# Linformer attention feeding a maxout layer: two products of batch 0 moved ahead of the first up product, and one projection moved to another PSUM bank

## The chip, the cores and the metric

The kernel runs on one core of one Trainium2 chip. A core has a matrix engine (TensorE, in the profile PE, with its weight loads as PEld), a vector engine (VectorE, DVE), a scalar engine (ScalarE, ACT), a general one (GpSimd, POOL) and a queue engine (SyncE, SP). Each runs its own list of instructions in order; they wait for each other through semaphores. TensorE writes into PSUM, which this kernel divides into eight banks. The metric is the device time of one execution in microseconds (us); the time before is 332.01 us, the median of nine runs (329.39 to 332.21).

## The reference

Eight batches, eight heads, 1024 positions, head size 64. Keys and values are projected along the sequence to 64 rows, then comes ordinary attention over these 64, and the heads side by side (8192 rows of 512) go into a two-branch maxout layer:

```python
k_proj = einsum('ks,bhsd->bhkd', E, k)
v_proj = einsum('ks,bhsd->bhkd', F, v)
attn = softmax(q @ k_proj.T / 8)
x = (attn @ v_proj), heads side by side      # 8192 x 512
g = maximum(x @ w1, x @ w2)                  # 8192 x 1024
out = g @ w_out                              # 8192 x 512
```

## The kernel before

**Algebra.** max(a, b) is relu(a - b) + b. So with wd = w1 - w2 and m = w2 @ w_out, the output is relu(x @ wd) @ w_out + x @ m. wd is made by VectorE in four pieces of 256 columns (`step_wd`, L418), m by TensorE from transposed w2 (`step_w2t` L427, `step_m` L440). "Up" is x @ wd with relu, "down" the product with w_out and m. Batch 0 does its up products plainly (`up_slots`, L404): 16 blocks u0[0..7] and u1[0..7], four matmuls of 512 columns each; u0 reads the first 256 columns (j = 0) of each half of x, u1 the second (j = 1). From batch 1 on, up and down use seven block products in place of eight (`up_steps` L558, `down_steps` L636).

**Attention of one batch.** `step_kv` projects k and v (L180), `step_kpt` and `step_qt` transpose (L211, L237) for batches 0 and 1; later batches have their q transposed by DMA (L249). Heads are taken in two groups g of four, positions in two parts j. For a pair (g, j): `step_sc` gives scores (L266) and their exponentials (L306), `step_dn` sums and logarithms of sums (L278, L312), `step_inv` their inverses (L316), and `step_at` the products with v (L278: 16 small matmuls) and the multiplies by the inverses (L329: two per pair) that write x, called xt. Later batches do the same in `step_group`.

**PSUM.** Four single banks, mm0 to mm3, are given out in rotation by `mm_bank()`; later they are named outright. Two double banks, the attention banks, come from `att_banks()`. `step_kv` and `step_at` take a flag `att`, which says from which of the two. With it, `step_kv` hands back its second half (the eviction of v, L196, and its copy, L200), to be issued after the next slot.

**Order.** The whole order is written out by hand. Lines L717 to L751 are batch 0's attention. Then a list `slots` gives the order of batch 0's up products, the w2 transposes, the m products and all later work; a second table hangs attention steps of the next batch behind given slots. Filler matmuls on a matrix of ones (`warm(n)`, L140) are issued at places of the first stage; nobody reads their result. `loads(1, "v", "q", "k")` issues three loads of later batches on POOL's queue (L102); v and q of batch 2 are loaded behind batch 1's `step_kv`. Stores (L651) and the DMA transposes (L249) share SP's queue.

Around the change, the program order of batch 0 is: products for (0, 0), products for (1, 0), the first piece of wd, u0[0], products for (0, 1), u0[1], products for (1, 1), three loads, the second piece of wd, u1[0], u1[1], u0[2], and so on.

Of the kernel before, what the change touches and what calls it, by code (L numbers as in the profile page):

```python
# [16 lines left out]
def kernel(  # L17
# [14 lines left out]
    B, H, S, D = q.shape  # L32
# [27 lines left out]
    def mm_bank(dtype=FP32, n=None):  # L60
        if n is None:
            n = turn.pop(0)
            turn.append(n)
        return ps.tile([128, 512 if dtype == FP32 else 1024], dtype, tag=f"mm{n}", name="mm_ps")

    def att_banks(dtype=FP32):
        return ps.tile(
            [128, 2, 512 if dtype == FP32 else 1024], dtype, tag="att", bufs=2, name="att_ps"
        )
# [27 lines left out]
    def load_all(t, b, n, src):  # L97
        alloc(t, n)
        load(t, n, src, b, 0, H)
# [37 lines left out]
    def warm(n):  # L137
        w_ps = mm_bank()
        for _ in range(n):
            nc.tensor.matmul(  # L140
                out=w_ps, lhsT=ones16[:, 0:128], rhs=ones16, start=True, stop=True
            )
# [145 lines left out]
    def values_into(t, g, j, at_ps):  # L288
        for z in range(2):
            tiles_into(  # L290
                lambda o: at_ps[o][:, z * W : (z + 1) * W], t["ex", g, j],
                lambda rows, hh: t["vp"][rows, 4 * g + hh, z, :],
            )

    def new_xt(t):
        t["xt"] = xpool.tile([128, NP2, 2, HALF], FP16, tag="xt", name="xt_sb")

    def x_out(t, g, j):
        return t["xt"][:, 2 * g : 2 * g + 2, :, j * W : (j + 1) * W]
# [18 lines left out]
    def step_at(t, g, j, att=False):  # L318
        if "xt" not in t:
            new_xt(t)  # L320
        ld = t.pop(("ld", g, j))
        if att:
            both = att_banks()
            at_ps = [both[:, o, :] for o in range(2)]
        else:
            at_ps = [mm_bank() for _ in range(2)]
        values_into(t, g, j, at_ps)
        for o in range(2):
            nc.vector.tensor_tensor(  # L329
                out=x_out(t, g, j)[:, :, o, :],  # L330
                in0=at_ps[o].rearrange("q (z n) -> q z n", z=2),
                in1=ld[:, o, None, :].broadcast_to([128, 2, W]),
                op=ALU.mult,
            )
# [63 lines left out]
    def up_slots(t, j):  # L398
        t["gt", j] = gt = gpool.tile([128, NFB, HALF], FP16, tag="gt", name="gt_sb")
        for fb in range(NFB):  # L400
            def up(fb=fb):
                h_ps = mm_bank()
                for r in range(NDC):
                    nc.tensor.matmul(  # L404
                        out=h_ps,
                        lhsT=wd_sb[:, r, fb * 128 : (fb + 1) * 128],
                        rhs=t["xt"][:, r, :, j * W : (j + 1) * W],
                        start=(r == 0), stop=(r == NDC - 1),
                    )
                if fb < 3:  # L410
                    nc.scalar.activation(out=gt[:, fb, :], in_=h_ps, func=ACTF.Relu)
                else:
                    nc.vector.tensor_scalar_max(gt[:, fb, :], h_ps, 0.0)
            yield up


    def step_wd(f0):
        nc.vector.tensor_tensor(  # L418
            out=wd_sb[:, :, f0 : f0 + 256], in0=w1_sb[:, :, f0 : f0 + 256],
            in1=w2_sb[:, :, f0 : f0 + 256], op=ALU.subtract,  # L420
        )

    def step_w2t(f0):
        ps_t = mm_bank(FP16)
        for f in range(2):
            for r in range(NDC):
                nc.tensor.transpose(  # L427
                    out=ps_t[:, (f * NDC + r) * 128 : (f * NDC + r + 1) * 128],
                    in_=w2_sb[:, r, f0 + f * 128 : f0 + (f + 1) * 128],
                    identity=ident16,  # L430
                )
        fb = f0 // 128
        nc.scalar.copy(
            out=w2t_sb[:, fb : fb + 2, :].rearrange("q f m -> q (f m)"), in_=ps_t
        )
# [281 lines left out]
    t = tiles[0]  # L717
# [31 lines left out]
    step_inv(t, 1, 1)  # L749
    step_at(t, 1, 0)  # L750
    step_wd(0)  # L751


    load_all(tiles[1], 1, "k", k)
    u0, u1 = [*up_slots(t, 0)], [*up_slots(t, 1)]
    wt = [lambda f0=f0: step_w2t(f0) for f0 in range(0, DF, 256)]
    wd = [lambda f0=f0: step_wd(f0) for f0 in range(0, DF, 256)]
    f = lambda s, *a: lambda: s(tiles[0], *a)

    def loads(b, *names):  # L760
        for n in names:
            b_ = b + (n == "k" and b < 2)
            if b_ < B:
                load_all(tiles[b_], b_, n, {"k": k, "v": v, "q": q}[n])

    slots = [
        (0, u0[0]), (None, f(step_at, 0, 1)), (1, u0[1]), (None, f(step_at, 1, 1)),
        (None, lambda: loads(1, "v", "q", "k")),
        (None, wd[1]), (2, u1[0]), (3, u1[1]), (4, u0[2]), (None, wt[0]), (5, u0[3]),
        (None, wd[2]), (None, wt[1]), (6, u1[2]), (7, u1[3]), (8, u0[4]), (9, u0[5]), (None, wd[3]),  # L770
        (None, wt[2]), (10, u1[4]), (11, u1[5]), (12, u0[6]), (13, u0[7]), (None, wt[3]),
        (14, u1[6]), (15, u1[7]),
# [28 lines left out]
    def at_slot(key, s, *a):  # L801
        steps.setdefault(key, []).append(lambda: s(*a))
# [11 lines left out]
    t = tiles[1]  # L814
    at_slot((0, 19), new_attn, t)
    at_slot((0, 19), lambda: turn.__setitem__(slice(None), [2, 3]))
    for n, x in enumerate((
        "kv", "", "kpt", "qt00 qt10", "", "sc00 sc10", "qt01", "qt11", "",
        "dn00 in00 dn10 in10", "", "", "at00 AT10 sc01", "", "",
    )):  # L820
        key = ("P", 0, (n - 1) // 2, (n - 1) % 2) if n else (0, 19)
        for name in x.split():
            if name[0] == "k":
                if name == "kpt":
                    at_slot(key, step_kpt, t, 0, H, True)
                else:
                    at_slot(key, step_kv, t)
                    at_slot(key, loads, 2, "v", "q")
            else:
                g, j = int(name[2]), int(name[3])  # L830
                s_ = {"qt": step_qt, "sc": step_sc,
                      "dn": step_dn, "in": step_inv, "at": step_at, "AT": step_at}[name[:2]]
                args = (4 * g, 4, 2 * j, 2 * j + 2) if name[:2] == "qt" else (g, j)
                at_slot(key, s_, t, *args, *([True] if name[:2] == "AT" else []))
        if n in (1, 5):
            at_slot(key, step_t, 1, (0, 1) if n == 1 else (2, 3))
        if 6 <= n < 10:
            at_slot(key, sums_x, U[0, 1], ((2, 0, 1, 3)[n - 6],))


    t = tiles[2]
# [8 lines left out]
    for b in range(3, B):  # L850
        t = tiles[b]
# [75 lines left out]
```

## Time and profile before

| | |
|---|---|
| median of nine runs | 332.01 us |
| profiled execution, its own time | 330.6 us |
| span in the profile (first to last instruction) | 328.8 us |
| TensorE busy | 318.0 us, 97% |
| VectorE busy | 239.6 us, 73% |
| ScalarE busy | 201.0 us, 61% |
| mean granted TensorE clock | 0.994 |
| DMA queues | 53.14 MB moved, mean 162 GB/s |

The page gives busy time, the chain of work that ended last, and the groups of instructions by line. A row of the timeline has the start in us from the span's start, a length, the engine, the line, the operation with its tiles, a count, and in brackets how long the engine stood idle before it and what ended that. A row with a count covers its instructions from the first start to the last end; small matmuls overlap in it. A table by stretches gives each engine's busy time, then the granted clock and the DMA share. Landing times count from the issue of a load on its queue.

### The profile page before, as it was taken

The numbers are of one execution on the slowest core, as the hardware profiler recorded it, in microseconds if no ns is written. First come the engines' busy times: TensorE is split into PE (matmuls) and PEld (weight loads), VectorE is DVE, ScalarE is ACT, GpSimd is POOL, SyncE is SP. The second block draws the span as 40 slices with busy tenths as digits, with TensorE's granted clock in tenths as the row PEclk, the third lists the DMA queues.
The fourth block names the chain that finished last, engine by engine and source line by source line (L and its number), as shares of the span: only waits on it lengthen the run. The fifth ranks groups of instructions, "written<-read, shape, count | busy, mean of one in ns | idle before, by whom it ended". The sixth has DMA issues, their size and how long they took to land.

```text
span 328.8 us, 9007 instructions
## 1 busy us (share of the span) xinstructions
PE 318.0 (97%) x3852; PEld 248.7 (76%) x3852; DVE 239.6 (73%) x424; ACT 201.0 (61%) x359; POOL 37.2 (11%) x56
## 2 busy tenths in 40 slices
PE   7986999999999999999999999999999999999994
PEld 3542546777888788878887888878887888888883
DVE  1246698995968779677968787777967796969572
ACT  2263422566776577767776677667776777765541
POOL 8555002003000030003000200003000000000000
PEclk9899999999999999999999999999999999999999
DMA  8999999997997789995999799897999220212132
GB/s 151 202 199 202 208 207 199 207 221 132 193 243 168 152 123 225 196 212 89 203 236 198 101 172 242 199 175 106 221 189 211 64 99 32 98 34 98 33 129 96
DMA packets 74680, 53.14 MB, mean 162 GB/s; under 512 B 29456, under 2 KB 74512, under 8 KB 74640
## 3 DMA queue, kind: packets, MB, share of 16 engines
q0 software_dynamic: 29376, 28.31, 54.6%
q1 hardware_dynamic: 45264, 24.25, 30.4%
q8 instruction: 30, 0.49, 0.6%
q14 instruction: 10, 0.08, 0.1%
HBM read 57.15 MB, written 16.78 MB: 225 GB/s over the span
## 4 chain that ended last, share of the span: by engine, by line
PE 89%; DVE 6%; DMA 2%; issue 1%; ACT 1%; SPq 0%; DVEq 0%
PE mm_ps L636 43%; PE mm_ps L558 25%; PE mm_ps L404 4%; PE att_ps L180 3%; PE att_ps L278 3%; PE mm_ps L266 3%; PE mm_ps L440 2%; PE mm_ps L180 2%; DMA big<-in_F_dram 2%; PE mm_ps L140 1%; DVE xt_sb L329 1%; DVE qt_sb L242 1%; DVE gt_sb L573 1%; DVE o_sb L660 1%; PE mm_ps L237 1%
## 5 line engine op out<-in xcount | busy, mean ns | idle before, releaser
L529 ACT COPY p_sb<-mm_ps 128x512 f32<-128x512 f32 x172 | 97.2, 594 | 43.0 <-PE mm_ps L558 30.6
L636 PEld LDWEIGHTS <-big 128*128 128x128 f16 x768 | 73.6, 98 | 12.0 <-issue 3.5
L636 PE MATMUL mm_ps<-T_sb,big 128*128 128x256 f16 x576 | 77.9, 273 | 0.0
L573 DVE TENSOR_TENSOR gt_sb<-mm_ps,p_sb 128x512 f16<-128x512 f32 x56 | 38.5, 688 | 45.8 <-PE mm_ps L558 42.6
L558 PE MATMUL mm_ps<-big,big 128*128 128x256 f16 x336 | 50.4, 273 | 0.0
L558 PEld LDWEIGHTS <-big 128*128 128x128 f16 x448 | 43.8, 98 | 5.3 <-issue 0.2
L636 PEld LDWEIGHTS <-gt_sb 128*128 128x128 f16 x384 | 35.7, 98 | 9.6 <-issue 5.4
L636 PE MATMUL mm_ps<-wo_sb,gt_sb 128*128 128x256 f16 x256 | 42.9, 273 | 0.1
L558 PEld LDWEIGHTS <-wd_sb 128*128 128x128 f16 x336 | 32.9, 98 | 4.2 <-issue 0.4
L558 PE MATMUL mm_ps<-xt_sb,wd_sb 128*128 128x256 f16 x224 | 33.6, 272 | 0.2 <-ACT ex_sb L355 0.2
L355 ACT ACTIVATE ex_sb<-mm_ps 128x512 f16<-128x512 f32 x50 | 27.2, 597 | 9.6 <-PE att_ps L278 7.0
L381 DVE TENSOR_TENSOR xt_sb<-att_ps,ld_sb 128x1024 f16<-128x1024 f32 x26 | 31.7, 1219 | 0.1
L660 DVE TENSOR_TENSOR o_sb<-mm_ps,p_sb 128x512 f32<-128x512 f32 x32 | 21.9, 684 | 11.0 <-PE mm_ps L636 7.6
L636 PE MATMUL mm_ps<-m_sb,xt_sb 128*128 128x256 f16 x128 | 24.4, 273 | 0.0
L608 ACT ACTIVATE gt_sb<-mm_ps 128x512 f16<-128x512 f32 x28 | 16.8, 600 | 8.7 <-PE mm_ps L558 8.7
L519 DVE TENSOR_TENSOR big<-gt_sb 128x1024 f16<-128x1024 f16 x32 | 21.9, 684 | 0.2
L576 DVE TENSOR_SCALAR gt_sb<-gt_sb 128x512 f16<-128x512 f16 (+1 forms) x56 | 20.4, 365 | 1.9
L636 PE MATMUL mm_ps<-T_sb,gt_sb 128*128 128x256 f16 x128 | 21.5, 273 | 0.0
L636 PE MATMUL mm_ps<-wo_sb,big 128*128 128x256 f16 x128 | 21.5, 273 | 0.0
L636 PEld LDWEIGHTS <-xt_sb 128*128 128x128 f16 x192 | 18.8, 98 | 2.2
L229 POOL COPY junk<-kpt_sb 1x1 f16<-1x1 f16 x5 | 0.9, 176 | 164.6 <-DMA kpt_sb<-kp_sb 164.6
L573 DVE TENSOR_TENSOR gt_sb<-p_sb 128x512 f16<-128x512 f32 x28 | 19.1, 681 | 0.0
(87 smaller groups left out, 429.2 us busy)
## 6 DMA issues: line engine op xcount, KB each, us to landing
out_dram<-o_sb SPq DMA_DIRECT2D x63, 256.0 KB, 2.5
k_sb<-in_k_dram POOLq DMA_DIRECT2D x7, 1024.0 KB, 10.1
v_sb<-in_v_dram POOLq DMA_DIRECT2D x7, 1024.0 KB, 17.5
q_sb<-in_q_dram POOLq DMA_DIRECT2D x7, 1024.0 KB, 22.5
k_sb<-in_k_dram POOLq DMA_DIRECT2D x4, 256.0 KB, 6.9
q_sb<-in_q_dram POOLq DMA_DIRECT2D x4, 256.0 KB, 8.0
v_sb<-in_v_dram POOLq DMA_DIRECT2D x2, 512.0 KB, 11.8
big<-in_moe_w_dram POOLq DMA_DIRECT2D x8, 128.0 KB, 9.8
```

Source lines behind the costliest of these rows:

```text
L180: nc.tensor.matmul(out=kv_ps[r * KP : (r + 1) * KP, 0:n], lhsT=eft[:, i, c, :], rhs=t[w][:, h0:h1, c, :], start=(c == 0), stop=(c == NC - 1),)
L355: nc.scalar.activation(out=t["ex", g, j][:, e, :], in_=banks[e], func=ACTF.Exp, scale=scale)
L381: nc.vector.tensor_tensor(out=x_out(t, g, j).rearrange("q z o n -> q o z n"), in0=at_ps.rearrange("q o (z n) -> q o z n", z=2), in1=ld[:, ...
L404: nc.tensor.matmul(out=h_ps, lhsT=wd_sb[:, r, fb * 128 : (fb + 1) * 128], rhs=t["xt"][:, r, :, j * W : (j + 1) * W], start=(r == 0), stop= ...
L519: nc.vector.tensor_tensor(out=S(i), in0=x, in1=y, op=op)
L529: copy(out=x, in_=bank)
L558: nc.tensor.matmul(out=bank[:, m * W : (m + 1) * W], lhsT=w_[:, n_, (2 * d + m) * 128 : (2 * d + m + 1) * 128], rhs=a[:, n_, :], start=(n ...
L573: nc.vector.tensor_tensor(out=c_blk(j, c), in0=two(x), in1=two(y), op=ALU.add)
L576: nc.vector.tensor_scalar_max(ap, ap, 0.0)
L608: nc.scalar.activation(out=out, in_=in_, func=ACTF.Relu)
L636: nc.tensor.matmul(out=bank[:, i * CH : (i + 1) * CH], lhsT=a(c)[:, i * 128 : (i + 1) * 128], rhs=w_(c), start=(n is not None and m == (lo ...
L660: nc.vector.tensor_tensor(out=o_sb, in0=two(x), in1=two(y), op=ALU.add)
```

## The change

The products of (0, 1) and (1, 1) are taken out of the slots and issued at the end of batch 0's attention, behind the first piece of wd in program order and ahead of u0[0]; they write attention banks in place of four rotating ones. Four filler matmuls follow them. The loads and the second piece of wd keep their places relative to their own engines' work: the order on VectorE, ScalarE, POOL and SP is the same as before. Batch 1's `step_kv` takes an attention bank too; its second half is issued one slot later.

```diff
     step_at(t, 1, 0)
     step_wd(0)
+    step_at(t, 0, 1, True)
+    step_at(t, 1, 1, True)
+    warm(4)
...
     slots = [
-        (0, u0[0]), (None, f(step_at, 0, 1)), (1, u0[1]), (None, f(step_at, 1, 1)),
-        (None, lambda: loads(1, "v", "q", "k")),
-        (None, wd[1]), (2, u1[0]), (3, u1[1]), (4, u0[2]), (None, wt[0]), (5, u0[3]),
+        (0, u0[0]), (1, u0[1]), (None, lambda: loads(1, "v", "q", "k")), (2, u1[0]), (3, u1[1]),
+        (None, wd[1]), (4, u0[2]), (None, wt[0]), (5, u0[3]),
...
-                    at_slot(key, step_kv, t)
+                    at_slot(key, step_kv, t, 0, H, "kv", True)
```

## The prediction

> **What bounds the kernel now.** I read the page first (busy shares, then the chain that ended last), then the timelines of TensorE and VectorE around the edit, then every arrival that work after the edit depends on.
>
> ```profile
> PE 318.0 (97%) x3852; PEld 248.7 (76%) x3852; DVE 239.6 (73%) x424; ACT 201.0 (61%) x359; POOL 37.2 (11%) x56
> PE 89%; DVE 6%; DMA 2%; issue 1%; ACT 1%; SPq 0%; DVEq 0%
> ```
>
> TensorE is the bound: busy 97% of the span, 89% of the chain. Whatever shortens its idle time early moves all later work, unless something on a clock of its own (a transfer) takes over. The edit lies where the page still shows gaps. The timeline of TensorE there (start, length, group, idle before it):
>
> ```profile
> 24.12 0.41 PE L278 MATMUL mm_ps<-ex_sb,vp_sb 64*32 64x256 f16 x16 [0.72 <-DVE vp_sb L193]
> 26.62 1.04 PE L404 MATMUL mm_ps<-xt_sb,wd_sb 128*128 128x512 f16 x4 [2.09 <-DVE wd_sb L418]
> 27.59 0.41 PE L278 MATMUL mm_ps<-ex_sb,vp_sb 64*32 64x256 f16 x16
> 27.93 1.04 PE L404 MATMUL mm_ps<-xt_sb,wd_sb 128*128 128x512 f16 x4
> 28.90 0.41 PE L278 MATMUL mm_ps<-ex_sb,vp_sb 64*32 64x256 f16 x16
> 29.48 0.59 PE L404 MATMUL mm_ps<-xt_sb,wd_sb 128*128 128x512 f16 x2 [0.17 <-DVE xt_sb L329]
> 30.79 2.32 PE L404 MATMUL mm_ps<-xt_sb,wd_sb 128*128 128x512 f16 x10 [0.72 <-DVE xt_sb L329]
> ```
>
> It idles 2.09 us until VectorE has made the first quarter of wd (L418); only then come the two last products with v (L278, at 27.59 and 28.90), each behind an up product (L404). The third up product, u1[0], needs the multiplies of those very products and waits 0.17 and 0.72 us. From 30.79 on TensorE runs without a gap until 57.9. VectorE shows the same from its side:
>
> ```profile
> 25.88 0.68 DVE L418 TENSOR_TENSOR wd_sb<-big,big 128x1024 f16<-128x1024 f16 x1
> 28.14 2.60 DVE L329 TENSOR_TENSOR xt_sb<-mm_ps,ld_sb 128x512 f16<-128x512 f32 x4 [1.58 <-PE mm_ps L278]
> 30.66 0.68 DVE L418 TENSOR_TENSOR wd_sb<-big,big 128x1024 f16<-128x1024 f16 x1
> ```
>
> After wd it stands 1.58 us for the late products, then needs 2.60 us for the four multiplies; their end, 30.74, releases 30.79.
>
> **The change, part by part.**
>
> *Products with v ahead of the first up product.* Both go into the gap. Their inputs are ready: the attention pairs they write were last read by ScalarE's L312, which ended at 22.3 and 24.4. After the block at 24.12, issued by about 24.46, two blocks at 0.34 each (27.59 to 27.93) end near 25.2. The first up product still waits for wd: 26.62, unchanged. VectorE's order is unchanged too, so the multiplies now follow wd at once: 26.56 + 2.60 = 29.16. TensorE meanwhile needs from 26.62 two up products at 0.865 (the x10 row: the next group begins 2.16 us later, 0.216 each), to 28.35, and the first half of u1[0], to 28.78; it then waits 0.4 us for the multiplies and takes the second half at 29.2 instead of 30.79. **Gain 1.6 us.** Counted on TensorE: 2 x 0.45 of products taken out from between the up products (1.31 from 26.62 to 27.93 less 0.865), plus 0.17 and 0.72 of waits with some 0.2 of refilling around them, less the 0.4 that stays.
>
> *Next on VectorE*, wd's second quarter moves from 30.66 to about 29.1, and is needed by u0[2], now at 29.2 + 0.43 + 0.865 = 30.5. Its last weights were issued at 21.55 and took 5.9 us: 27.5, in time. It now falls beside POOL's load issue of 29.14 to 30.01. Row: the first wd piece ran at 25.88 while POOL issued without a break (25.10 to 27.80) and took 0.68 like the one at 38.97 with POOL idle. The Trainium skill (SBUF — State Buffer, "Who interferes with whom") has a rule against this edit: a VectorE operation with two SBUF inputs contends for a shared port pair with a GpSimd instruction reading SBUF, and the loser blocks fully. If issuing counted as that, wd would end at 30.01 + 0.68 = 30.7, u0[2] would start 0.25 late, and the gain be 1.35. I take the row: no loss.
>
> *Four dummies* (L140): 4 x 0.216 = 0.87 us, from 25.2 to 26.1, half a microsecond before 26.62. Covered by the wait for wd; without that cover they would cost 0.87, at half clock 1.73 (then ending near 27.0, 0.3 late). What can they bring? The rows of granted clock:
>
> ```profile
> 6.00:8.00 2.00, 1.86 (x11) 1.07 (x10) 0.68 (x1) 0.24 (x1) 2.00 (x4) 0.93 1.20 180
> 8.00:10.00 2.00, 2.00 (x9) 1.17 (x8) 0.00 (x0) 0.34 (x1) 1.18 (x3) 0.50 1.20 191
> 10.00:12.00 2.00, 2.00 (x16) 0.60 (x15) 0.71 (x2) 0.00 (x0) 1.38 (x2) 0.72 1.24 204
> 25.00:26.00 1.00, 0.00 (x0) 0.00 (x0) 1.00 (x3) 0.47 (x1) 1.00 (x3) 1.00 1.38 200
> ```
>
> (Stretch, length, busy times of PE, PEld, DVE, ACT, POOL, then the granted clock.) Across the gap the clock stayed at 1.00, so here they bring 0. The skill (TensorE: Matmul & The Clock Gate, Part 1) has the clock halved after an idle window of about 3.4 us in a free-running count; a 2.09 us gap is shorter, so its rule also gives 0. But the dip of 7 to 11 us contradicts it as a limit: half clock although TensorE was busy 1.86 of 2 us just before. That dip cost 0.14 + 1.00 + 0.56 = 1.7 us of clock, so in executions with another phase the gap may cost up to that. Bounds for the dummies: 0 to 1.7 us gained; I take 0 (the 25:26 row is nearest).
>
> *v, q and k loads.* Same order on POOL, past the same instructions; they wait for buffers free since 23.2. SP's queue keeps its order. Nothing.
>
> *Batch 1's k and v into an attention bank.* The same 16 products (1.89 us at 51.3) into a bank whose last reader, a multiply of the last products, ends at 29.2. The evictions (kp 0.58, vp 0.69, its copy 0.75) keep order; the second half is issued one slot later in program order, behind products that sit on another engine. Before, the bank was one of the rotation, and the transposes of q at about 56.0 waited for its eviction, over at 54.5: a wait removed that had ended. The rotation's phase shifts, each bank still reused after three others. 0 us, bounds -0.1 to +0.2 (the only idle near: 0.18 at 58.50, on a qt copy).
>
> *Do later arrivals allow it?* With all of TensorE 1.6 us earlier:
>
> ```profile
> q_sb<-in_q_dram POOLq DMA_DIRECT2D x1, 1024.0 KB, 24.7
> 55.53 1.06 PE L237 MATMUL mm_ps<-ident,q_sb 128*128 128x128 f16 x16
> 77.63 0.18 POOL L229 COPY junk<-qt_sb 1x1 f16<-1x1 f16 x1 [22.44 <-DMA qt_sb<-q_sb]
> 79.80 0.40 PE L266 MATMUL mm_ps<-qt_sb,kpt_sb 64*32 64x256 f16 x16
> ```
>
> Batch 1's q was issued at 28.02 and lands at 52.7; wanted at 55.53, then at 53.9: 1.2 spare. Batch 1's v lands at 26.86 + 20.8 = 47.7, wanted at 51.3, then 49.7. Batch 2's v and q are issued sooner (53.45 to 51.9) but queue behind k, which lands at 29.14 + 28.6 = 57.7, so q still lands at 69.9 and the transposed q at about 77.6; its first scores move from 79.80 to 78.2: **0.6 spare, the narrowest place**. Beyond it, loads for batch 3 start behind that gate and are read past 100 us.
>
> *Sum.* -1.6 + 0 + 0: span 328.8 to 327.2, the profiled execution 330.6 to 329.0. The nine runs before have a median of 332.01, 1.4 above the profiled one; the same difference gives **330.4**.
>
> **Rivals.**
>
> (a) *Transfers take the gain.* Loads kept the DMA engines full until 70 us. If in the usual 332 us execution batch 2's q lands a microsecond or more later than here, 79.80 doesn't move fully; gain 0 to 0.6, time 331.4 to 332.0. For: 0.6 spare. Against: TensorE would be later there too, and keep its distance.
>
> (b) *The gap costs clock in the usual execution.* The 1.4 us between profiled run and median would be a half-clock stretch caused by the gap; the dummies end it. Gain 1.6 + 1.4, time 329.0. For: the dip can cost 1.7 and changes phase freely. Against: not seen at the gap in this profile.
>
> (c) *Slower: half-clock stretches elsewhere.* The new order makes TensorE's activity fall otherwise on the clock's count, in the up products from 26.6 on. Price 1.7 each: one gives 332.1 (no change), two 333.8. Slower from 1.6 + 1.0 = 2.6 us of lost clock. Against: clock 1.00 in every row after 12 us, with more idle time than the new order has.
>
> (d) *It doesn't do what it says.* If the multiplies came later on VectorE, or a product waited for an attention pair, 332.0. The compiled order has the products directly behind the last block, the multiplies directly behind wd.
>
> **How the numbers follow.** Main case 0.60 (own range 329.7 to 331.0: port rule, spare time, spread of runs); (a) 0.12; (b) 0.10; (c) 0.15, of which 0.04 ends within no change; (d) 0.03. What a measurement here can tell from no change is 0.3%, 1.0 us. Faster: 0.60 of the main case less 0.04 for runs falling short, plus (b), plus 0.02 of (a): 0.68. Same: 0.04 + 0.10 + 0.04 + 0.03 = 0.21. Slower: the rest of (c), 0.11. Range 328.7 to 332.5: from (b) to just past one dip.
>
> **What would show it.** Right: the products at 24.5 to 25.2, dummies behind, the first up product still at 26.6, the multiplies at 26.5 to 29.2, one wait of some 0.4 us inside u1[0], then no gap; everything from there 1.6 us earlier, the scores at 78.2 without a wait. Wrong: the first up product after 26.7, wd's second piece over 0.7, a wait for qt near 78, or granted clock below 1.00 after 12 us.

## The result

The changed kernel takes 329.14 us (median of 18 runs, 327.75 to 331.13) where the kernel before takes 331.95 us (median of 55 runs): ratio 0.993, 95% interval 0.9913 to 0.9947, so 2.3 us faster, between 1.8 and 2.9. The forecast was 330.4, a gain of 1.6; the direction and the range held, the size was short by 0.7 us in the ratio and by 1.3 us in the median.

### The profile after

Its profiled execution took 327.73 us with a span of 326.0. The page's busy shares and its chain (shares of the span):

```profile
PE 317.4 (97%) x3856; PEld 248.9 (76%) x3856; DVE 239.5 (73%) x424; ACT 201.0 (62%) x359; POOL 37.0 (11%) x56
PE 86%; DMA 6%; DVE 4%; POOL 2%; issue 1%; ACT 1%; DVEq 0%; POOLq 0%
```

TensorE does the same work, and the four dummies, in a shorter span. In the chain, 6% now runs over transfers, where it was 2%: loads of batch 0's v (4%) and of the weights (2%), issued ahead of the edit. The timeline of TensorE around the edit:

```profile
22.99 0.41 PE L278 MATMUL mm_ps<-ex_sb,vp_sb 64*32 64x256 f16 x16 [0.52 <-DVE vp_sb L193]
23.22 0.62 PE L278 MATMUL att_ps<-ex_sb,vp_sb 64*32 64x256 f16 x32
23.77 1.04 PE L140 MATMUL mm_ps<-ones 128*128 128x512 f16 x4
25.50 4.71 PE L404 MATMUL mm_ps<-xt_sb,wd_sb 128*128 128x512 f16 x20 [0.68 <-DVE wd_sb L418]
30.04 0.61 PE L427 MATMUL mm_ps<-ident,big 128*128 128x128 f16 x8
```

The two moved blocks are the x32 row at 23.22, the dummies follow, and the first five up products run as one group. The first w2 transpose of the kernel before was here:

```profile
32.95 0.61 PE L427 MATMUL mm_ps<-ident,big 128*128 128x128 f16 x8
```

From the products of (1, 0) to the first w2 transpose it is 30.04 - 22.99 = 7.05 us; before, 32.95 - 24.12 = 8.83. I call this distance *the stretch*. It is **1.78 us** shorter. VectorE over the same time:

```profile
24.75 0.68 DVE L418 TENSOR_TENSOR wd_sb<-big,big 128x1024 f16<-128x1024 f16 x1
25.35 2.48 DVE L329 TENSOR_TENSOR xt_sb<-att_ps,ld_sb 128x512 f16<-128x512 f32 x4
27.75 0.68 DVE L418 TENSOR_TENSOR wd_sb<-big,big 128x1024 f16<-128x1024 f16 x1
```

The 1.58 us in which it stood for late products are gone, and the second piece of wd, beside POOL's load issues of 27.83 to 29.64, still takes 0.68.

The two spans differ by 2.8 us, but 1.1 of that is not the change: the products of (1, 0) start 1.13 us earlier already, ahead of anything that was edited. The granted clock accounts for it (columns as in the prediction, then the DMA share and GB/s):

```profile
6.00:8.00 2.00, 2.00 (x13) 1.20 (x12) 0.69 (x1) 0.08 (x1) 2.00 (x4) 1.00 1.19 188
8.00:10.00 2.00, 2.00 (x16) 0.98 (x16) 0.42 (x1) 0.51 (x1) 1.73 (x3) 1.00 1.23 199
24.00:26.00 2.00, 1.32 (x7) 0.47 (x6) 2.00 (x5) 0.16 (x1) 2.00 (x3) 1.00 1.41 199
```

This execution has no dip to half clock at 8 to 11 us, and the second projection of k already runs 1.4 us earlier (13.48 against 14.85); 0.3 is then lost to a wait for v's load. The code up to there is the same in both kernels, so that is chance from one execution to the next. Comparing the two profiles end to end would mistake it for part of the gain.

Farther on, the lines that answer to the arrivals in the prediction:

```profile
q_sb<-in_q_dram POOLq DMA_DIRECT2D x1, 1024.0 KB, 24.6
52.62 1.06 PE L237 MATMUL mm_ps<-ident,q_sb 128*128 128x128 f16 x16
76.94 0.18 POOL L229 COPY junk<-qt_sb 1x1 f16<-1x1 f16 x1 [24.64 <-DMA qt_sb<-q_sb]
76.90 0.40 PE L266 MATMUL mm_ps<-qt_sb,kpt_sb 64*32 64x256 f16 x16
```

Batch 1's q (issued at 27.83, landed at 52.4) was there 0.2 us before its transposes at 52.62. Here almost nothing is left to spare. Batch 2's first scores (the last line) started 2.9 us earlier than before and without a wait. That the gate (L229) opened at the same moment means nothing for them: it reads the last head, and the first scores need only the first four (see the account below).

### The profile page after: what moved, and what is told of

Its sections match the earlier page's. It is cut to its first block, busy times and chain, and to the rows that moved or that the text cites. A ratio compares the mean times of both kernels' runs of the same rounds, so it can differ in the third digit from the quotient of the medians.

```text
span 326.0 us, 9015 instructions
## 1 busy us (share of the span) xinstructions
PE 317.4 (97%) x3856; PEld 248.9 (76%) x3856; DVE 239.5 (73%) x424; ACT 201.0 (62%) x359; POOL 37.0 (11%) x56
## 4 chain that ended last, share of the span: by engine, by line
PE 86%; DMA 6%; DVE 4%; POOL 2%; issue 1%; ACT 1%; DVEq 0%; POOLq 0%
PE mm_ps L636 43%; PE mm_ps L558 26%; DMA v_sb<-in_v_dram 4%; PE att_ps L180 4%; PE mm_ps L404 4%; PE att_ps L278 3%; PE mm_ps L266 3%; PE mm_ps L440 2%; DMA big<-in_moe_w_dram 2%; POOL q_sb L102 1%; POOL k_sb L102 1%; DVE gt_sb L573 1%; DVE o_sb L660 1%; PE mm_ps L427 1%; DVE qt_sb L242 0%
## 5 line engine op out<-in xcount | busy, mean ns | idle before, releaser
L229 POOL COPY junk<-kpt_sb 1x1 f16<-1x1 f16 x5 | 0.9, 177 | 162.5 <-DMA kpt_sb<-kp_sb 162.5
```

## The experiments

**What was to be told apart.** Theory A: the gain is the multiplies that follow wd at once, 1.6 to 1.8 us. Theory B, the prediction's rival (b): part of it is clock that the gap used to cost. Theory C: part of it is the other bank for batch 1's projection. P stands for the moved products, D for the four dummies, K for the projection's bank; the changed kernel is P+D+K. Ratios are to the kernel before, timed beside each experiment on the same chip. *Lost clock* is one minus the mean granted clock, times the span, as a mean over a kernel's runs; over 144 runs the kernel before lost 2.31 us, over 19 runs the changed one lost 0.95.

Lost clock is a sign, not a price: part of it lies where TensorE has nothing to do. The changed kernel's profile lost about 1 us of clock, all of it behind the last matmul, which ended at 321.6:

```profile
324.00:325.00 1.00, 0.00 (x0) 0.00 (x0) 0.00 (x0) 0.00 (x0) 0.00 (x0) 0.50 0.27 93
```

Over the 144 runs of the kernel before, a straight line through time and lost clock has a slope of 0.42 us per us.

### P alone

```diff
     step_wd(0)
     step_at(t, 0, 1, True)
     step_at(t, 1, 1, True)
-    warm(4)
...
-                    at_slot(key, step_kv, t, 0, H, "kv", True)
+                    at_slot(key, step_kv, t)
```

(This diff is against the changed kernel.)

> The two products ahead of the first up product, in attention banks; no dummies, batch 1's projection in its old bank. Theory A (the whole gain is the multiplies that follow the first piece of wd without a gap): as fast as the changed kernel, 1.6 to 1.8 us under the kernel before, ratio 0.9945 to 0.9955. Theory B (part of the measured 2.3 us is clock that the dummies save in the gap): only 0.8 to 1.2 us, ratio 0.996 to 0.998. Theory C (the attention bank for the projection brings the rest): 1.8 us at most, with the projection's own run showing what is missing.

Measured: 329.44 us, ratio 0.9923 (0.9893 to 0.9952), lost clock 1.38 us over 10 runs, stretch 7.04 us. The products alone carry a gain as large as that of the whole change. Theory B's smaller figure for this run is outside the interval; theory A's lies just inside it.

### D alone

```diff
     step_wd(0)
+    warm(4)
```

(Against the kernel before.)

> The kernel before with four dummies behind the first piece of wd, ahead of the first up product, and nothing else. Theory A: they lie in the wait for wd (2.09 us for 0.87 us of work), 0 us, ratio 1.000. Theory B: they keep the clock up in the usual execution, 0.5 to 1.5 us faster, ratio 0.9955 to 0.9985.

Measured: 331.29 us, ratio 0.9989 (0.9964 to 1.0014); lost clock only 0.47 us over 14 runs, stretch 8.82 us. The dummies do save clock, about 1.8 us of it, but the time hardly moves. The interval leaves both theories open; the next experiment doubles the number of dummies.

### D with eight dummies

```diff
     step_wd(0)
+    warm(8)
```

(Against the kernel before.)

> The kernel before with eight dummies (1.73 us) in the 2.09 us gap ahead of the first up product, and nothing else: the dummies' effect with twice the dose. Theory B: mean lost clock falls from 2.7 us to under 0.6 us, and since a half-clock stretch behind the gap cost 1.0 us where a profile showed one, the time falls by 0.6 to 1.3 us, ratio 0.996 to 0.998. Theory A: lost clock may fall, the time stays, ratio 0.999 to 1.001.

Measured: 331.21 us, ratio 0.9985 (0.997 to 1.0001), lost clock 0.69 us over 22 runs. Again clock saved with little to show for it. The timeline of TensorE in this kernel tells where it goes:

```profile
51.01 0.38 PE L180 MATMUL mm_ps<-k_sb,eft 128*64 128x512 f16 x1 [0.67 <-ACT m_sb L444]
```

Batch 1's projection waits 0.67 us for ScalarE's copy of the last m block. The dummies take one rotating bank, which turns the rotation by one, and the projection, which takes a fixed bank (number 2), now gets the one that the last m product has just filled. The same wait stands in the profile with four dummies. Before, it got another m block's bank, long empty.

### K alone

```diff
-                    at_slot(key, step_kv, t)
+                    at_slot(key, step_kv, t, 0, H, "kv", True)
```

> The kernel before with batch 1's projection of k and v in an attention bank, its second half one slot later, and nothing else. Theory A: 0 us, ratio 1.000, since the wait that it removes had ended 1.5 us before it was asked for. Theory C: 0.5 to 1 us faster, ratio 0.997 to 0.9985.

Measured: 332.02 us, ratio 1.0011 (0.9985 to 1.0037). Alone the bank is worth nothing, as theory A had it. Its profile had a chance find, in the stretches of 2 us:

```profile
24.00:26.00 2.00, 0.30 (x2) 0.19 (x3) 1.64 (x3) 0.34 (x1) 2.00 (x3) 1.00 1.42 200
26.00:28.00 2.00, 2.00 (x23) 0.67 (x22) 0.78 (x2) 0.60 (x1) 2.00 (x3) 0.78 1.23 201
28.00:30.00 2.00, 2.00 (x20) 0.43 (x19) 0.99 (x2) 0.60 (x1) 1.84 (x3) 0.50 1.18 175
30.00:32.00 2.00, 1.48 (x7) 0.55 (x6) 1.40 (x3) 0.51 (x1) 0.00 (x0) 0.87 1.20 160
```

This kernel has the old gap of 2.09 us, and behind it, in the up products, the clock falls to half. The early dip is missing here. Its stretch is 9.81 us, 0.98 longer than the 8.83 of the kernel before at full clock: what rival (b) described does happen, and the profile of before had merely not caught it.

### D and K together

```diff
     step_wd(0)
+    warm(4)
...
-                    at_slot(key, step_kv, t)
+                    at_slot(key, step_kv, t, 0, H, "kv", True)
```

(Against the kernel before.)

> The kernel before with the four dummies and batch 1's projection in an attention bank; the products stay where they were. In the two runs with dummies alone the dummies' bank turned the rotation by one, and the projection then waited 0.67 us for the last m copy, which hid a gain in clock. Theory B': without that wait the dummies are worth 0.5 + 0.67, 0.8 to 1.4 us: ratio 0.996 to 0.9975, mean lost clock under 0.8 us, no wait ahead of the projection. Theory A (dummies worth nothing): ratio 0.999 to 1.001.

Measured: 330.38 us, ratio 0.9959 (0.9944 to 0.9974), lost clock 0.88 us over 22 runs, no wait ahead of the projection; stretch 8.83 us, unchanged. So without moving a product, dummies and bank are worth 1.4 us (0.9 to 1.9). The stretch at full clock is no shorter, which makes the clock the likeliest thing that they bring. The profiled execution can't show it: at 331.57 us it was one of this kernel's slowest, with the early dip and a wait far behind the edit, for a transposed k:

```profile
223.80 0.41 PE L266 MATMUL mm_ps<-qt_sb,kpt_sb 64*32 64x256 f16 x16 [0.93 <-DMA kpt_sb<-kp_sb]
```

Five of the fourteen profiles have this wait, of 0.9 to 1.1 us (here, and with P alone, D alone, one product moved, and rotating banks with dummies). How often each kernel meets it was not measured, so it stays open as a part of the differences between kernels.

### P and D, the projection in a rotating bank

```diff
-                    at_slot(key, step_kv, t, 0, H, "kv", True)
+                    at_slot(key, step_kv, t)
```

(Against the changed kernel.)

> The changed kernel with batch 1's projection back in a rotating bank (products and dummies as changed). The five banks taken less turn the rotation as the dummies alone do, so the projection waits 0.67 us for the last m copy: 0.5 to 0.7 us slower than the changed kernel, ratio 0.9945 to 0.9955, the wait seen in the profile. If the bank does not matter: ratio 0.992 to 0.994 and no wait.

Measured: 329.62 us, ratio 0.9939 (0.9915 to 0.9963), stretch 7.05. The interval doesn't separate it from the changed kernel, but the profile has the wait that was expected, and a second one:

```profile
PE mm_ps L180 <- ACT m_sb L444: 0.7, 1, 0.7
PE mm_ps L237 <- DMA q_sb<-in_q_dram: 0.5, 1, 0.5
```

(Who waited for what: us in total, times, longest.) The first is the bank. The second is batch 1's q, which landed at 54.6 here; TensorE had to wait for it even after losing 0.7 us.

### P and K, no dummies

```diff
     step_at(t, 1, 1, True)
-    warm(4)
```

(Against the changed kernel.)

> The changed kernel without its four dummies. Theory A (multiplies alone): ratio as the changed kernel, 0.993 to 0.9945, stretch from the first products of (1, 0) to the first transpose of w2 7.05 us as there. Theory B (gap costs clock): the products themselves fill 0.4 us of the gap, so some of the clock comes back: mean lost clock (one minus the granted clock, times the span) between the 0.95 us of the changed kernel and the 2.7 us of the kernel before, and 0.2 to 0.5 us slower than the changed kernel, ratio 0.9935 to 0.996.

Measured: 329.31 us, ratio 0.992 (0.9889 to 0.9951), lost clock 1.97 us over 8 runs. The profile shows the gap's dip once more:

```profile
25.88 6.00 PE L404 MATMUL mm_ps<-xt_sb,wd_sb 128*128 128x512 f16 x20 [1.65 <-DVE wd_sb L418]
```

And the stretches of 2 us around it:

```profile
24.00:26.00 2.00, 0.35 (x22) 0.12 (x2) 2.00 (x4) 0.61 (x2) 2.00 (x4) 0.89 1.39 197
26.00:28.00 2.00, 2.00 (x6) 0.62 (x6) 2.00 (x4) 0.19 (x1) 2.00 (x3) 0.50 1.26 202
28.00:30.00 2.00, 2.00 (x9) 0.85 (x8) 0.82 (x2) 1.00 (x2) 2.00 (x3) 0.76 1.12 156
```

A gap of 1.65 us suffices for it, and the same 20 matmuls take 6.00 us instead of 4.71: 1.29 us. Yet over its runs this kernel is no slower than the changed one. With 8 runs and an interval of 1 us to either side, the 0.2 to 0.5 us that was expected can't be seen or denied.

### Only one of the two products moved

```diff
     step_at(t, 0, 1, True)
-    step_at(t, 1, 1, True)
...
-        (0, u0[0]), (1, u0[1]), (None, lambda: loads(1, "v", "q", "k")), (2, u1[0]), (3, u1[1]),
+        (0, u0[0]), (1, u0[1]), (None, f(step_at, 1, 1, True)), (None, lambda: loads(1, "v", "q", "k")), (2, u1[0]), (3, u1[1]),
```

(Against the changed kernel.)

> The changed kernel, but only the products of (0, 1) stand ahead of the first up product; those of (1, 1) follow the second up product. Theory A: VectorE does two of the four multiplies early and the other two about 28.7 to 30.0 on the time scale of the profile before, so u1[0] gets its second half at 30.1 instead of 29.2 or 30.8: 0.7 us under the kernel before, ratio 0.998. Theory B or C (the gain is not in the multiplies): close to the changed kernel, ratio 0.993 to 0.995.

Measured: 330.19 us, ratio 0.995 (0.9935 to 0.9965), 1.7 us, with 0.66 us of lost clock over 22 runs; stretch 8.38 us. The stretch at full clock is only 0.45 us shorter than before (0.7 was expected: the second product comes behind the second up product and its multiplies wait for it). The time gained is larger than the stretch by 1.2 us, and this kernel too has the gap filled with dummies: about what dummies and bank bring on their own (1.4). Theory A's ratio of 0.998 lies outside the interval.

### 20 dummies

```diff
-    warm(4)
+    warm(20)
```

(Against the changed kernel.)

> The changed kernel with 20 dummies in place of four: 16 x 0.216 = 3.46 us more in TensorE's order, of which 0.7 us fit into the rest of the gap and 0.2 us into the wait inside u1[0]. If the dummies are free only by their cover: 2.5 us slower than the changed kernel, ratio to the kernel before 1.000 to 1.002. If something later (a load) takes up part of the delay: less, ratio 0.996 to 0.999.

Measured: 330.92 us, ratio 0.9992 (0.9976 to 1.0007), stretch 9.43 us: 2.4 longer than in the changed kernel, 2.0 us in the ratio. Dummies are free only as long as the wait for wd covers them; beyond that nearly their whole length is paid.

### The moved products in rotating banks, with and without dummies

```diff
-    step_at(t, 0, 1, True)
-    step_at(t, 1, 1, True)
+    step_at(t, 0, 1)
+    step_at(t, 1, 1)
```

(Against the changed kernel; the second run leaves out `warm(4)` as well.)

> The changed kernel with the two moved products written into rotating banks, as before, in place of attention banks. The first two up products then reuse banks that the multiplies of (0, 1) have to empty: they start about 0.6 us later and follow VectorE, which still ends its multiplies at the same time. Theory A: 0.2 to 0.4 us slower than the changed kernel, ratio 0.994 to 0.996. If the attention banks are the essence of the change: most of the gain gone, ratio over 0.997.

> The two products moved into rotating banks, no dummies, projection in an attention bank. In the run with dummies the dummies' own bank had to wait for a multiply, which held the up products back. Without them the first up product waits for the first multiply of (0, 1), about 0.5 us past wd, and u1[0] ends 0.3 us later than in the changed kernel: stretch from the products of (1, 0) to the first transpose of w2 7.3 to 7.5 us at full clock against 7.05, ratio 0.993 to 0.996. If the attention banks matter by themselves: ratio over 0.997.

Measured with dummies: 331.42 us, ratio 0.9991 (0.9969 to 1.0014), nearly all of the gain gone; the expectation was wrong. Its timeline of TensorE:

```profile
22.97 0.63 PE L278 MATMUL mm_ps<-ex_sb,vp_sb 64*32 64x256 f16 x32 [0.52 <-DVE vp_sb L193]
24.27 0.27 PE L278 MATMUL mm_ps<-ex_sb,vp_sb 64*32 64x256 f16 x1 [0.67 <-DVE xt_sb L329]
24.87 0.41 PE L278 MATMUL mm_ps<-ex_sb,vp_sb 64*32 64x256 f16 x15 [0.33 <-DVE xt_sb L329]
26.07 1.70 PE L140 MATMUL mm_ps<-ones 128*128 128x512 f16 x4 [0.79 <-DVE xt_sb L329]
```

The products of (1, 1) wait for the banks of (1, 0), and the dummies, which need a rotating bank too, wait 0.79 us for a multiply of (0, 1), then take 1.70 us instead of 1.04, most of it at half clock, in front of the first up product. The dummies' own bank was the step that my expectation left out. Without dummies: 330.26 us, ratio 0.9962 (0.9941 to 0.9982), the same waits in front of the up products, lost clock 2.39 us over 22 runs, stretch 9.10 us with the dip in it. The ratio ended just above the expected band. With the same products in attention banks and no dummies the ratio was 0.992. So without the attention banks nearly all of the gain is lost with dummies, and about half of it without.

### Less TensorE work ahead of the loads

The sum of two of the four m blocks is cut to its first half.

```diff
-        for fb in range(NFB):
+        n_fb = NFB if r < 2 else NFB // 2
+        for fb in range(n_fb):
             nc.tensor.matmul(
                 out=m_ps, lhsT=w2t_sb[:, fb, r * 128 : (r + 1) * 128], rhs=wo_sb[:, fb, :],
-                start=(fb == 0), stop=(fb == NFB - 1),
+                start=(fb == 0), stop=(fb == n_fb - 1),
```

(Against the changed kernel.)

> The changed kernel with half of the sum left out in two of the four blocks of m (8 matmuls of 512 columns, 1.73 us, less TensorE work ahead of batch 1's projection; m is then half a sum in two blocks). It asks whether the load chain is the next limit. If transposed q of batch 2 (landing at about 76.9, scores at 76.90 in the changed kernel's profile) is it: a wait appears ahead of those scores and the gain is 0 to 0.7 us against the changed kernel, ratio 0.991 to 0.993. With the 0.6 us to spare that the prediction named: 0.6 us. If no load is in the way: 1.7 us, ratio 0.987 to 0.989.

Measured: 328.86 us, ratio 0.9904 (0.9867 to 0.994): of 1.73 us left out, 0.9 come through in the ratio and 0.3 in the median, with a wide interval (6 runs). Its waits on TensorE:

```profile
PE att_ps L180 <- DMA v_sb<-in_v_dram: 1.3, 1, 1.3
PE mm_ps L237 <- DMA q_sb<-in_q_dram: 0.6, 1, 0.6
```

In this execution more than what was saved is waited for again, 1.9 us. So here the loads are the next limit, though at batch 1's v and q and not at batch 2's q, where I looked for it. The interval over the runs is too wide to say how much of the 1.73 us they usually take.

## Why the prediction was right, and where it was short

**Products into the gap, multiplies at once behind wd: right, and sized nearly right.** 1.6 was forecast, the stretch shows 1.78. Two small terms were off. The four multiplies took 2.48 us, not 2.60, because they ran back to back: before, the second pair had to wait for its products (from rotating banks they took 2.48 too). And VectorE started them at 25.35, some 0.08 us before wd's end at 25.43. The first up product came where wd releases it, and of the wait of 0.4 that was forecast inside u1[0] about 0.2 was left (the 20 matmuls from 25.50 to 30.04: 4.54 - 20 x 0.216).

**wd's second piece beside POOL's issue: right.** The port rule of the Trainium skill (SBUF — State Buffer, "Who interferes with whom") would have made it longer only if issuing a load counted as an SBUF read of GpSimd; it took 0.68 beside an issue in progress.

**Dummies, "I take 0": the reason failed, the number is not refuted.** The reason was the clock row of one profile, in which the dip had fallen at 8 to 11 us. The gap does cost clock, as rival (b) said: in the profiles with the old or little-filled gap and no early dip (K alone; P and K), and with rotating banks, the dip sat behind the gap each time; where the gap was filled it never did, except where the dummies themselves were held back. Without the moved products, dummies and bank are worth 1.4 us. But beside the moved products the dummies brought nothing that could be measured: 0.9923 (P) and 0.992 (P and K) without them, 0.9939 (P and D) and 0.993 (the change) with them, though lost clock fell from 1.38 to 0.92 and from 1.97 to 0.95.

**Where the other half microsecond came from: open.** The change measured 2.3 us (1.8 to 2.9), the stretch accounts for 1.78, and the interval nearly reaches down to that; the interval of the products alone, 2.6 (1.6 to 3.6), includes it. Clock is the likeliest rest. Compare runs at a mean clock of 0.999 or more: 9 of 144 before, with a median of 329.6 us, and 9 of 19 of the changed kernel, with 328.3. That is 1.3 us at equal clock, and the remaining 1 us would be that the changed kernel keeps its clock far more often. This is an estimate from few runs, which were not timed side by side. That clock and products (1.4 and 2.6) do not add up in the change would fit loads that take the rest: batch 1's q landed between 52.4 and 54.7 us in the fourteen profiles, and the changed kernel, which wants it at 52.62, was profiled with the earliest of all. No run shows it waiting there.

**The projection's bank, "0 us": right alone, wrong in company.** I saw that the rotation's phase shifts and argued that each bank is still reused after three others. But the projection takes a fixed bank right behind four m products, and a shift by one gives it the bank of the last. 0.67 us would have been waited there, as in three profiles (both with dummies alone; P and D); the attention bank avoids it.

**Later arrivals: right for batch 1's q, misread for batch 2's.** Batch 1's q was forecast with 1.2 us to spare; 2.9 us ahead of the profile before, the changed kernel's profile had 0.2, and P and D waited 0.5. The "narrowest place", 0.6 us at batch 2's first scores, was not one. It was read from the gate at 77.63, but the gate reads the last head, which comes with the second of two transposes, and these scores use heads of the first. In the run of P and D the scores began first:

```profile
78.44 0.40 PE L266 MATMUL mm_ps<-qt_sb,kpt_sb 64*32 64x256 f16 x16
79.14 0.18 POOL L229 COPY junk<-qt_sb 1x1 f16<-1x1 f16 x1 [25.54 <-DMA qt_sb<-q_sb]
```

In the changed kernel the first transpose was issued at 70.04 and took at most 4.9 us, so these scores, at 76.90, had about 2 us to spare. In none of the fourteen profiles does TensorE wait for batch 2's q. Rival (a) was right in kind, at batch 1's v and q: they cost time in two profiles (P and D; half of m).

**Sum and range.** 330.4 was short, most likely because the main case was built on one execution's clock. Its own range, 329.7 to 331.0, missed 329.14; the outer range held it, because rival (b), at 329.0, had been given a place in it. Rivals (c) and (d) did not occur: over its runs the changed kernel lost less clock than before, and the profile shows the order that was described.

## What to carry to other kernels

Work whose inputs are ready belongs into a wait that can't be shortened, above all when a second engine's next stretch depends on it; price it on that second engine, as here 1.58 us of VectorE's idle time. An operation that takes a bank from a rotation moves every later user of it: look for the first user behind a run of fresh products, since dummies alone gained about half a microsecond, not clear of zero, until the projection had a bank of its own. A clock row from one execution says what happened there, not what usually happens: take the mean clock of many runs, look where in the span the clock is lost, and compare profiles by the distance between two fixed instructions rather than by their spans. Before calling an arrival narrow, check which part of the transfer is needed there: the instruction that shows a landing may wait for another part.

## What the runs showed of the hardware

- Gaps of 1.65 and 2.09 us on TensorE, with shorter ones just ahead, were followed by about 3.4 us at half clock (P and K; K alone; for P and K the rows above give 0.44 + 2.00 + 0.96); the 20 matmuls behind the first took 6.00 us instead of 4.71. In both kernels with rotating banks a row of waits of 0.3 to 0.8 us was followed by the same. The Trainium skill (TensorE: Matmul & The Clock Gate, Part 1) speaks of an idle window of about 3.4 us; here no single gap was that long.
- The dip falls early (8 to 11 us) or behind the gap, by chance: up to there the code is the same. Each of the five profiles without the added dummies had exactly one, twice early and three times late. Of the nine with them six had none, two an early one, and one, with rotating banks, a late one.
- Batch 1's q, issued at 27.6 to 28.5 us in all fourteen kernels behind the same loads, landed between 52.4 and 54.7 us: 2.3 us apart, as much as the whole change is worth.
